# Block-sparse attention and a gated MLP on one core: two key loads change queues, pair 0's keys come in two parts, and the written order is a new one

## The chip, the cores and the metric

The kernel runs on one core of one Trainium2 chip. The metric is device microseconds of one execution, from the first instruction to the last store's arrival. Of the kernel before, three timed runs are given, with a median of 262.63 us (262.12 to 263.25). A core has a matrix engine (TensorE, PE in the profile), VectorE (DVE), ScalarE (ACT), GpSimd (POOL) and SyncE (SP). Each works through its own list of instructions in order. DMA transfers are issued from SP, ACT or POOL; an issue takes time on the list of the engine that issues it.

## The reference: what is computed

```python
# attention: batch 4, 8 heads, 768 positions, head width 64, blocks of 32
scores = scale * q @ k.T                       # per batch and head
mask = neighbours(+-1 block) | first/last block row or column | 3 sampled key blocks per query block
scores = where(mask, scores, -1e9)
attn = exp(scores - max); attn /= attn.sum(-1) + 1e-9
a = attn @ v
# MLP on the 3072 tokens, width 512, hidden width 2048
x = a.transpose(0, 2, 1, 3).reshape(3072, 512)
h = x @ w_in
out = (h / (1 + exp(-beta * h))) @ w_out       # float32
```

The mask is the same for every batch and head; it depends on `sampled_blocks`, a list of 24 x 3 integers that is read from memory.

## The kernel before, in words

**Tiling.** Two heads make a pair; there are 16 pairs (4 batches x 4). A pair's queries come in two tiles, one of 256 and one of 512, and a pair with one of its query tiles is called a unit: units 0 to 3 are the first 256 queries of pairs 0 to 3, units 4 to 7 their other 512, and so on to unit 31. Keys come in six chunks of 128. A unit has score steps (`sc` in `tile_steps`): a step is a double PSUM bank with 1024 columns. In units 0 to 3 a step covers two key chunks, so such a unit has three steps. ScalarE takes the exponential of each step (`ex`, tile `et`). VectorE multiplies the result with the 0/1 mask (`mk`). TensorE forms the weighted values (`av`), VectorE normalises (`norm`), and the result is turned into `x`.

**Masks in the first units.** In units 0 to 3 the mask isn't multiplied in. There TensorE adds -30000 to masked scores before the score product, with a one-hot matrix (`onehot`) against `shut_qk`. So those scores need `onehot`, `shut_qk`, and the turned keys `kX` and queries `qX`.

**Loads and turns.** A load (`add_load`) brings fp32 keys, queries or values into a staging tile (`st`, or `es`, which lies in the later `g` tiles). A cast makes fp16 of them (VectorE or GpSimd). For the first four pairs TensorE turns chunks of 128 by 128, and VectorE or ScalarE copies the turned chunks out of PSUM. Later pairs are turned by a DMA. `IN_PARTS` cuts the keys of pairs 0 and 1 into parts. `SPLIT_Q` cuts the queries of these pairs: first the 256 that units 0 and 1 need, then the rest (`add_rest`). One load, the one that `BESIDE` names, is issued by ScalarE; the others are issued by SP.

**The mask's own chain.** `emit_first` issues the load of the sampled list on ScalarE's queue and makes `identity`, the index tables and `onehot`. In `add_mask`, three VectorE instructions (`mb`) make the block mask from the list, a matmul (`mt`) spreads it, a copy (`mtc`) makes `mask_q`, and `neg` makes `shut_qk`. Three matmuls (`km`) and three copies (`kmc`) make the full mask `mask01`, which units from 4 on use. VectorE's list begins with `mb`.

**The MLP.** For each group of 256 or 512 tokens there are 16 hidden products (`hp`). ScalarE takes a tanh (`th`), VectorE multiplies (`gm`, tile `g`), and output products (`pr`) follow in a scheme with seven half-size products, whose sums on VectorE are `sg`; weight differences for them (`tw`, tile `w_mix`) are made once. `w_in` and `w_out` are loaded by GpSimd after the load that `GATE` names has landed.

**What sets the order.** `STEPS` is the order, written out by hand or by a search: `35S4` is node 35 on SP with buffer 4; the letters P, A, D, G, S stand for TensorE, ScalarE, VectorE, GpSimd and SP, and a number after a colon names a second TensorE node that shares the array with this one, each in one half of its rows (`in_halves`). Nodes are numbered in the order in which `add` makes them. The order fixes each engine's list; waits come from what a node reads and writes. Durations given to `add` and the times given as `at=` served the search and aren't in the program.

In the order before, SP's list starts: first queries of pair 1 (128 KB), keys of pair 1 chunks 0-1 (128 KB), all queries of pair 2 (384 KB), rest of pair 0's queries (256 KB), keys of pair 0 chunks 0-1 and 2-3 (128 KB each), first queries of pair 0 (128 KB), keys of pair 0 chunks 4-5 (128 KB), keys of pairs 2 and 3, queries of pair 3, `beta`, values. ScalarE's queue has the sampled list, then keys of pair 1 chunks 2-5 (256 KB). TensorE's list starts: `mt`, `km` for two groups, turns of pair 1's keys 2-5, keys 0-1 and queries, the third `km`, three score steps of unit 1, turns for pair 0 and of pair 2's queries, score steps of unit 0. ScalarE's starts: `onehot`, `mask_q`, `shut_qk`, two `kmc`, a copy of pair 1's keys, the third `kmc`, two exponentials of unit 1, a copy of pair 0's keys, the third exponential of unit 1, three of unit 0. Its first exponential takes the second score step that TensorE makes.

In the profile all instructions that are issued through the recording wrapper stand at one line, L200; they are told apart by their tiles. L362, L510, L392, L378 and L366 to L394 are in `add_load` and `emit_first`.

Of the kernel before, what the change touches and what calls it, by code (L numbers as in the profile page):

```python
# [43 lines left out]
0D 1P0 3A 4P7 8P6 2A 5A 9A 35S4 31S0 32D0 36D1 39S 40D 41P5 49S1 65S4 13S1 33P6 37P1 34A2 42D 6P5  # L44
7A 38D 21S 17S3 25S 96P3 94P1 95Ae 50D1 66G6 14G2 92P0 22D 18G3 26G 45S0 55S2 23P4 15P2 16D1 24D
59S3 10S 43S5 97A0 27P3 19P5 20D 29S4 28A 46G5 53S6 93A1 51P2 80P2 84P3 67P0 47P3 81A3 56G5 73G
82P2 74G 48D0 52D 60D1 68D 57P1 58D3 85A2 44G0 83A5 108P1 109Ac 106P3 107A6 104P2 61P1 62D 30D2
105A4 98P1 99P 116P3 87P0:86 100D0 101D0 117A8 63S7 75G 76G 69S8 54D1 118P1 188P2 189A9 86P 88D4
89D3 120P3 70G6 77G 78G 110P0 111P 112D2 11P4 12D 113D4 64D3 121A1 90P6 197P2 119Aa 194P0 79G
122P1 123P 91D0 124D4 198A3 195Ab 125D3 71P7 72D 191P2 192Ae 114P2 203P0 212P3 213A0 200P2 115D  # L50
190D 196D 201A1 204Aa 215P1 102P7 103D 126P6 127D 214D 193D 199D 149P5 128P4 216Ac 150A2 129A5
137P0 205D 202D 138A0 131P1 140P2 134P3 146P7 143P6 130D1 151D 217D 227P2 141A3 135A1 147A4 144A6
148D 145D 136D 132A5 228A2 218P3 219A4 161P3 167P4 158P5 162A1 168A4 159A2 139D 133D 229D 142D
220D 163D 155P2 224P3 156A3 225Ad 206P0:207 169D 160D 221P2 157D 222A8 226D 207P 244P1 245Ab 208Da
223D 209D4 164P6 173P7 170P4 165A3 246D 152P5 250P0 166D 171A1 174A4 230P1:231 153A0 251A7 175D
247P3 248A6 231P 154D 236S2 239S5 240D0 172D 288P0 232D1 259P2 260A1 256P3 237G3 238S1 233D1 257Ae
242S6 241S 268S7 176P23:182 276P2 277A2 252D 182P 183P:177 279P2 289Ac 285P3 280A5 177P 178P:184
286A3 258D 261D 253P2 271S3 249D 278D 291P0 356D 254Aa 357D 360D 281D 290D 255D 274S8 300S0 282P3
184P 179P 210P4 185P 283A0 292A4 287D 284D 293D 262P0:263 269G1 358D 361D 359D 211A1 180A1 186A0
# [63 lines left out]
1289D 1181S 1180S 1294A0 1296D 1299P 1301P 1302A1 1300D 1297D 1298D 1303P 1304D 1305P 1306D 1313S  # L123
1312S 1307A 1311D 1308P 1309A 1314S
"""
N_PEMASK = 4
ROWS6 = False
N_XPE = 8
SHUT = 30000.0
# [104 lines left out]
def kernel(  # L234
# [11 lines left out]
    nc = tc.nc  # L246
# [111 lines left out]
    def emit_first():  # L358
# [4 lines left out]
        for load in beside:  # L363
            load()
# [721 lines left out]
```

## Time and profile before

| what | value |
|---|---|
| median of three runs | 262.63 us (262.12 to 263.25) |
| the profiled execution's own time | 262.88 us |
| its span, first to last instruction | 261.1 us |
| TensorE busy | 249.6 us, 3767 matmuls |
| VectorE busy | 226.2 us, 445 instructions |
| ScalarE busy | 213.7 us, 288 instructions |
| GpSimd busy | 34.8 us, 50 instructions |
| moved by DMA | 36.81 MB, 141 GB/s over the span |

The profile shows one execution. Times in a timeline are microseconds from the start of the span; one line can stand for several instructions of one kind, with the first start and the time from there to the last end. Text in square brackets is idle time before the instruction and what ended it. Busy time of TensorE is modelled, so a busy TensorE isn't a TensorE at its peak.

### The profile page before, as it was taken

To read this page: it belongs to the slowest core of one execution; us is meant where nothing else is said; L and a number is where in the kernel's file an instruction comes from. 1 tells how busy PE (TensorE), PEld (TensorE's weight loads), DVE (VectorE), ACT (ScalarE), POOL (GpSimd) and SP (SyncE) were. 2 spreads that over 40 slices of the span, in tenths; PEclk is the share of its full clock that TensorE was granted. 3 is DMA by queue.
4 is the path that set the end of the run, shared out by engine and by line. 5 is a ranking of instruction groups with operands and counts; after the bars stand their busy time and mean duration, and the time that the engine had idled before them with its cause. 6 is when DMAs were issued, how large, how long until landed. Compare 5 with 4: busy or idle time off the path is not lost.

```text
span 261.1 us, 8802 instructions
## 1 busy us (share of the span) xinstructions
PE 249.6 (96%) x3767; PEld 171.8 (66%) x3767; DVE 226.2 (87%) x445; ACT 213.7 (82%) x288; POOL 34.8 (13%) x50
## 2 busy tenths in 40 slices
PE   5998799999989999999999999999999999999995
PEld 1675575564467976468876457856757986568894
DVE  4366998988999999989999999999999888589683
ACT  5699999999999997899898989975899874675241
POOL 3346001045220005210300200001100000000000
PEclk9999999999999999999999999999999999999999
DMA  6999994969756599931933999460050314100042
GB/s 202 340 342 175 207 198 85 280 167 262 178 194 189 175 121 246 172 133 35 261 83 73 251 147 253 57 137 0 3 183 4 22 23 173 22 3 0 3 160 81
DMA packets 50154, 36.81 MB, mean 141 GB/s; under 512 B 29748, under 2 KB 46660, under 8 KB 50116
## 3 DMA queue, kind: packets, MB, share of 16 engines
q1 hardware_dynamic: 46128, 31.80, 48.8%
q0 software_dynamic: 3680, 4.19, 9.8%
q8 instruction: 29, 0.48, 0.8%
q10 hardware_dynamic: 308, 0.26, 0.3%
q14 instruction: 9, 0.07, 0.1%
HBM read 27.27 MB, written 6.29 MB: 129 GB/s over the span
## 4 chain that ended last, share of the span: by engine, by line
PE 83%; DVE 11%; DMA 1%; ACT 1%; issue 1%; POOL 1%; SPq 0%; DVEq 0%; ACTq 0%
PE sc L200 83%; DVE et L200 5%; DVE g L200 3%; DMA st<-in_k_dram 1%; DVE xst L200 1%; ACT et L200 1%; DVE s L200 1%; DVE recip L200 0%; POOL s L200 0%; POOL va L200 0%; DVE kX L200 0%; ACT t_sb L200 0%; DVE va L200 0%; DVE x L200 0%; SPq L510 0%
## 5 line engine op out<-in xcount | busy, mean ns | idle before, releaser
L200 ACT ACTIVATE et<-sc 128x1024 f16<-128x1024 f32 x144 | 139.8, 1035 | 10.0 <-PE sc L200 8.5
L200 PE MATMUL sc<-x,w_in_sb 128*128 128x512 f16 (+2 forms) x504 | 92.1, 352 | 1.1 <-ACT et L200 0.5
L200 DVE TENSOR_TENSOR et<-et,mask 128x960 f16<-128x960 f16 x132 | 83.2, 670 | 1.4 <-ACT et L200 1.2
L200 ACT ACTIVATE t_sb<-sc,beta_c_sb 128x512 f16<-128x512 f32 (+1 forms) x112 | 65.1, 641 | 21.4 <-PE sc L200 19.4
L200 DVE SCALAR_TENSOR_TENSOR g<-t_sb,sc 128x512 f16<-128x512 f16 (+1 forms) x112 | 63.5, 606 | 7.8 <-ACT t_sb L200 7.3
L200 PEld LDWEIGHTS <-w_in_sb 128*128 128x128 f16 (+1 forms) x504 | 42.9, 97 | 37.5 <-issue 4.7
L200 PEld LDWEIGHTS <-g 64*128 64x128 f16 (+1 forms) x700 | 49.1, 96 | 15.2 <-issue 3.3
L200 PE MATMUL sc<-w_out_sb,g 64*128 64x256 f16 (+3 forms) x568 | 55.6, 281 | 0.5 <-DVE xst L200 0.3
L200 PE MATMUL sc<-qX,kX 64*128 64x256 f16 (+1 forms) x384 | 50.6, 328 | 1.4 <-DVE g L200 0.8
L200 PEld LDWEIGHTS <-et 64*128 64x128 f16 (+1 forms) x1776 | 41.7, 95 | 8.6 <-issue 1.4
L200 PE MATMUL sc<-va,et 64*128 64x65 f16 (+1 forms) x1776 | 44.3, 191 | 0.8 <-DVE xst L200 0.3
L200 PEld LDWEIGHTS <-kX 64*128 64x128 f16 x384 | 19.7, 95 | 12.5 <-issue 7.5
L200 POOL CAST s<-st 128x768 f16<-128x768 f32 (+2 forms) x17 | 15.1, 905 | 87.4 <-PE sc L200 34.5
L200 PEld LDWEIGHTS <-s 64*128 64x128 f16 (+1 forms) x320 | 22.0, 97 | 6.0 <-issue 1.7
L200 PE MATMUL sc<-w_mix,s 64*128 64x256 f16 (+1 forms) x272 | 23.6, 270 | 0.0
L200 DVE TENSOR_TENSOR xst<-sc,recip 128x256 f16<-128x256 f32 (+1 forms) x32 | 17.8, 557 | 0.9
L200 POOL CAST va<-st 128x768 f16<-128x768 f32 x10 | 9.6, 968 | 59.0 <-DVE g L200 32.0
L200 ACT COPY osb<-sc 128x512 f32<-128x512 f32 (+3 forms) x19 | 10.0, 539 | 8.5 <-PE sc L200 7.5
L200 PE MATMUL sc<-w_mix,g 64*128 64x256 f16 (+3 forms) x128 | 15.6, 264 | 0.0
L200 DVE TENSOR_TENSOR osb<-osb,sc 128x512 f32<-128x512 f32 (+2 forms) x19 | 11.7, 618 | 2.6 <-PE sc L200 1.5
L200 DVE RECIPROCAL recip<-sc 128x4 f32<-128x4 f32 (+1 forms) x32 | 6.2, 193 | 8.0 <-PE sc L200 7.7
L200 DVE CAST s<-st 128x768 f16<-128x768 f32 (+2 forms) x15 | 7.7, 522 | 2.0 <-DMA st<-in_k_dram 2.0
(60 smaller groups left out, 94.8 us busy)
## 6 DMA issues: line engine op xcount, KB each, us to landing
out_dram<-osb SPq DMA_DIRECT2D x23, 256.0 KB, 2.4
st<-in_k_dram SPq DMA_DIRECT2D x12, 384.0 KB, 4.9
st<-in_q_dram SPq DMA_DIRECT2D x12, 384.0 KB, 5.1
st<-in_v_dram SPq DMA_DIRECT2D x12, 384.0 KB, 4.5
g<-in_v_dram SPq DMA_DIRECT2D x4, 384.0 KB, 6.9
w_in_sb<-in_moe_w_in_dram POOLq DMA_DIRECT2D x2, 512.0 KB, 7.1
w_in_sb<-in_moe_w_in_dram POOLq DMA_DIRECT2D x1, 1024.0 KB, 10.7
w_out_sb<-in_moe_w_out_dram POOLq DMA_DIRECT2D x2, 512.0 KB, 12.9
```

The lines of the kernel that those rows point to most:

```text
L200: r = f(*a, **kw)
```

## The change

The loads of the first key chunks (0-1) of pairs 1 and 0 are issued by ScalarE, in this sequence: keys of pair 1, the sampled list, keys of pair 0. The load of pair 1's chunks 2-5, which ScalarE issued, goes to SP. Pair 0's keys come in two parts (chunks 0-1 and 2-5) and not in three, so one load, one cast, one turn and one copy fewer are there, and the node numbers above that point go down by four. The copy that makes `onehot` moves from ScalarE to GpSimd, ahead of the small `ident32` cast. The rest of the queries of pairs 0 and 1 goes into the staging tile of the first part, and no longer into one of its own. `shut_qk` is made 384 columns wide (it was 128) and lies in the `s` tile, which nothing uses before the MLP; the first units still use its first 128 columns. `PE_MASKED` names the same units 0 to 3 with all their steps. The mask copies may no longer go to GpSimd (none did).

`STEPS` is a new order. SP now starts: keys of pair 1 chunks 2-5 (256 KB), first queries of pair 1 (128 KB), keys of pair 2 (384 KB), first queries of pair 0 (128 KB), keys of pair 0 chunks 2-5 (256 KB), queries of pair 3, queries of pair 2, keys of pair 3, rest of pair 0's queries, values, rest of pair 1's, `beta`. TensorE starts: `mt`, turns of pair 1's keys 0-1, keys 2-5 and queries, three `km`, score steps of unit 1 (the first of them on chunks 0-1), turns of pair 0's keys 2-5 (four chunks), keys 0-1 (two), queries (two), of pair 2's keys (six), score steps of unit 0. ScalarE starts: `mask_q`, `shut_qk`, copies of pair 1's keys 0-1 and 2-5, one `kmc`, two exponentials of unit 1, the copy of pair 0's keys 0-1, the third of unit 1, three of unit 0; its first exponential takes the first score step. VectorE starts: `mb`, casts of pair 1's keys 0-1, keys 2-5 and queries, the copy of the queries, the cast of pair 2's keys, one `kmc`, the cast of pair 0's keys 2-5, another `kmc`. GpSimd casts pair 0's queries and first keys.

Further on, TensorE's list keeps nearly the order that it had: the pairs of nodes that run in half arrays are the same and in the same sequence, but for the weighted values of unit 0, which no longer share the array (41 pairs, 42 before). VectorE has 19 casts (22 before), GpSimd 33 (31 before). The casts of the keys for units 6 and 8 are now on VectorE (`265D3`, `417D3`), and one of the weight differences, `355D`, stands a few places later; several casts of units 13 to 23 have left VectorE. At the very end the narrow last product (`1306P5`, node 1310 before) stands after the wide one.

```diff
-0D 1P0 3A 4P7 8P6 2A 5A 9A 35S4 31S0 32D0 36D1 39S 40D 41P5 49S1 65S4 13S1 33P6 37P1 34A2 42D 6P5
-7A 38D 21S 17S3 25S 96P3 94P1 95Ae 50D1 66G6 14G2 92P0 22D 18G3 26G 45S0 55S2 23P4 15P2 16D1 24D
+27S0 35S 0D 1P0 28D0 29P7 36D 37P2 31S4 13S1 41S0 3A 2A 32D5 33P4 30A2 34D 17S3 21S 55S3 45S1 18G4
+14G1 4P0 6P1 8P3 38A 51S2 7A 88P3 90P2 89A0 42D2 5D 91A8 22D 9D 46G3 69G 70G 92P0 23P2 15P3 19P4
...
+181P 176A0 264S2 267S6 270S4 408P3 393P2 258P0:259 182A1 280D 354D 357D 265D3 358D 291P1:290 259P
...
+312D 316P2 317A2 313P0 424P3 337P13:319 271G2 395D 407D 417D3 314A4 425A2 318D 430P2 319P 431A3
...
+1304P 1308S 1306P5 1305A 1307D 1310S
...
-N_PEMASK = 4
+PE_MASKED = {0: 6, 1: 6, 2: 6, 3: 6}
-BESIDE = ("k", 1, 2)
-COPY384 = {"ACT": 395, "DVE": 465, "POOL": 480}
-EARLY = ("k2", "q2", "k3", "q3", "v0", "v1", "v2", "v3", "r1")
+BESIDE = (("k", 1, 0), ("k", 0, 0))
+COPY384 = {"ACT": 395, "DVE": 465}
+EARLY = ("k2", "q2", "k3", "q3", "v0", "v1", "v2", "v3")
-IN_PARTS = {0: (0, 2, 4, 6), 1: (0, 2, 6)}
+IN_PARTS = {0: (0, 2, 6), 1: (0, 2, 6)}
...
-    shut_qk = persist.tile([P, P], FP16, name="shut_qk")
+    shut_qk = T["s"][0].rearrange("p a f q -> p (a f q)")[:, 0:NG * P]
...
+        beside[0]()
         nc.scalar.dma_start(out=sb_i32, in_=sb_lo)
-        for load in beside:
-            load()
+        for i in range(1, len(BESIDE)):
+            beside[i]()
...
+        nc.gpsimd.tensor_copy(out=onehot, in_=onehot_n.rearrange("b p g -> b g p"))
         nc.gpsimd.tensor_copy(out=ident32, in_=identity[0:16, 0:16])
...
-        nc.scalar.copy(out=onehot, in_=onehot_n.rearrange("b p g -> b g p"))
...
-                act.activation(out=shut_qk, in_=at(tb)[:, 0:P], func=AF.Copy, bias=-SHUT,
+                act.activation(out=shut_qk, in_=at(tb)[:, 0:NG * P], func=AF.Copy, bias=-SHUT,
                                scale=SHUT)
...
-        st, s16 = at_work or (staging(f"{nm}{x}" if lo == 0 else f"r{x}"), Buf("s16"))
-        load = add_load(nm, x, st, lo, hi, gate, lo > 0 if at_work else None)
+        st, s16 = at_work or (staging(f"{nm}{x}"), Buf("s16"))
+        more = lo > 0 if at_work else None
+        if nm == "q":
+            st, more = rest_of.setdefault(x, st), lo > 0
+        load = add_load(nm, x, st, lo, hi, gate, more)
...
-                                rhs=shut_qk[r].unsqueeze(1).to_broadcast([D, CG, P]),
+                                rhs=shut_qk[r, q0 // CG:(q0 + n) // CG].rearrange(
+                                    "b (g p) -> b g p", p=P).unsqueeze(1).to_broadcast(
+                                        [D, CG, ng, P]),
...
-            steps, ets = tile_steps(x, q0, n, i * NPAIR + j < N_PEMASK)
+            steps, ets = tile_steps(x, q0, n, PE_MASKED.get(i * NPAIR + j, 0))
```

More of the change, by code (lines that the diff above doesn't have):

```diff
@@ L470 @@
     prep = {}
[L472 to L473 removed]
+    w_in_of, w_out_of, loads, rest_of, begun = {}, {}, {}, {}, {}
+    last_load, begin, early_casts, beside = [], [], [], {}
     def add_weights():
```

189 lines of the change are left out of this document (94 added, 95 removed).

## The prediction

> **What bounds the kernel now.** I read the page first, for the chain of work that ended last; then the busy time by stretches, because a share over the whole span mixes stages; then the timeline of the first 14 us, where the change lies; then the landing times of single loads.
>
> ```profile
> span 261.1 us, 8802 instructions
> PE 83%; DVE 11%; DMA 1%; ACT 1%; issue 1%; POOL 1%; SPq 0%; DVEq 0%; ACTq 0%
> ```
>
> ```profile
> 0.00:9.40 9.40, 6.48 (x34) 2.96 (x36) 4.72 (x21) 4.14 (x8) 3.60 (x16) 1.00 0.80 236
> 9.40:40.00 30.60, 27.30 (x489) 20.16 (x483) 22.13 (x57) 30.28 (x43) 8.29 (x12) 1.00 1.14 245
> 40.00:100.00 60.00, 58.65 (x1053) 36.98 (x1047) 56.67 (x103) 57.59 (x71) 11.90 (x13) 1.00 0.77 180
> 120.00:258.00 138.00, 137.78 (x1986) 99.94 (x1983) 123.71 (x233) 104.41 (x144) 6.07 (x6) 1.00 0.39 90
> ```
>
> Columns of the stretches: length, then busy time of PE, PEld, DVE, ACT, POOL, clock, DMA share, GB/s. The chain is TensorE's for 83% of the span and VectorE's for 11%. TensorE idles 2.9 us before 9.4, 3.3 us from there to 40, and 1.35 us from 40 to 100. From 9.4 to 40 the full engine is ScalarE (30.28 of 30.60): it takes exponentials one after another. After 120 TensorE is full (137.78 of 138). So what ScalarE gains at its first exponentials moves the train to 40 us, and the rest follows if nothing in between takes it back. TensorE's work stays the same: the same matmuls, masked units and turned chunks.
>
> ```profile
> 0.74 0.66 ACTq L362 DMA_DIRECT2D sb_i<-in_sampled_blocks_dram  x1
> 1.26 0.45 SPq L510 DMA_DIRECT2D st<-in_k_dram  x1
> 1.42 0.41 ACTq L510 DMA_DIRECT2D st<-in_k_dram  x1
> 1.75 1.06 POOL L378 COPY g<-identity 64x384 f16<-64x384 f16 x2
> 1.86 1.28 ACT L392 ACT_TABLE_LOAD   x1 [1.86 <-issue]
> 2.25 0.16 DVE L200 CAST sb_f<-sb_i 24x3 f32<-24x3 int32 x1 [0.21 <-DMA sb_i<-in_sampled_blocks_dram]
> 3.16 0.51 ACT L392 COPY onehot<-g 128x384 f16<-128x384 f16 x1
> 3.32 0.50 PE L200 MATMUL sc<-g,mask 24*128 24x384 f16 x1 [0.24 <-DVE mask L200]
> 3.85 0.47 ACT L200 CAST mask_q<-sc 24x384 f16<-24x384 f32 x1 [0.18 <-PE sc L200]
> 4.22 0.26 ACT L200 ACTIVATE shut_qk<-sc 128x128 f16<-128x128 f32 x1
> 4.37 0.79 PE L200 MATMUL sc<-mask_q,onehot 24*128 24x384 f16 x2 [0.56 <-ACT mask_q L200]
> 5.12 0.83 DVE L200 CAST s<-st 128x256 f16<-128x256 f32 x3 [1.86 <-DMA st<-in_k_dram]
> 6.86 0.37 ACT L200 COPY kX<-sc 128x256 f16<-128x256 f16 x1 [1.12 <-PE sc L200]
> 7.28 0.55 DVE L200 CAST s<-g 128x768 f16<-128x768 f32 x1
> 7.53 0.40 PE L200 MATMUL sc<-shut_qk,onehot 64*128 64x256 f16 x2
> 7.99 0.72 DVE L200 CAST s<-st 128x256 f16<-128x256 f32 x1 [0.16 <-DMA st<-in_k_dram]
> 8.36 0.42 PE L200 MATMUL sc<-shut_qk,onehot 64*128 64x256 f16 x2
> 9.46 1.94 ACT L200 ACTIVATE et<-sc 128x1024 f16<-128x1024 f32 x2 [1.34 <-PE sc L200]
> 10.21 0.92 PE L200 MATMUL sc<-identity,s 128*128 128x128 f16 x8
> 11.67 2.86 ACT L200 ACTIVATE et<-sc 128x1024 f16<-128x1024 f32 x3
> 12.01 0.27 PE L200 MATMUL sc<-shut_qk,onehot 64*128 64x256 f16 x2
> 12.76 0.73 PE L200 MATMUL sc<-identity,s 128*128 128x128 f16 x10
> ```
>
> The gate of the start is the landing of pair 1's first keys: VectorE waits 1.86 us for it, until 5.12. Casts, turns and copies of 512 KB of pair 1 follow, and the first score step begins at 7.53. The second begins at 8.36, so a step takes 0.83; the first exponential, at 9.46, takes that second step: 1.10 after its begin. The fourth exponential, unit 0's first, stands at 11.67 + 0.97 = 12.64.
>
> ```profile
> st<-in_q_dram SPq DMA_DIRECT2D x1, 128.0 KB, 2.3
> st<-in_k_dram SPq DMA_DIRECT2D x1, 128.0 KB, 3.8
> st<-in_k_dram ACTq DMA_DIRECT2D x1, 256.0 KB, 3.9
> g<-in_q_dram SPq DMA_DIRECT2D x1, 384.0 KB, 4.6
> ```
>
> These are the first three loads of SP's queue (issued at 0.74, 1.26 and 1.76) and the key load of ScalarE's, with microseconds from issue to landing: 3.04, 5.06, 6.36 and 5.32.
>
> **The change part by part.**
>
> *Three issues on ScalarE.* 0.46 more than before (an issue of 128 KB on SP took 0.45), so the table load ends near 3.6 and not 3.14. ScalarE's next work comes at 5.1 (below): costs nothing; uncovered it would be 0.46.
>
> *The one-hot copy.* ScalarE loses 0.51, which nobody waited for. GpSimd does half of the partitions in 0.53 (1.06 for two), so it ends at 3.3 to 3.9, if the other read pattern doubles it. The first reader is a `km` at 5.85. Nothing.
>
> *The sampled list.* It is issued at 1.2 in place of 0.74. VectorE began on it 1.51 after the issue. Below that is 2.7; above, behind 128 KB on the same queue, 1.2 + 3.8 = 5.0. I take 3.5, nearer to the list's own row, since its packets are few. The three `mb` instructions take 1.0 (from 2.25 to just before the matmul at 3.32), and behind them on VectorE's list wait all the casts: 4.5. The spreading matmul adds 0.55, `mask_q` 0.47 from 5.1, and `shut_qk`, now as wide as `mask_q`, 0.47 in place of 0.26: 6.0. The copy of the first keys is then done at 6.4.
>
> *Pair 1's loads.* The last one needed is now the queries, second on SP behind 256 KB. Before, 256 KB of SP's queue had landed at 5.06 and 640 KB at 6.36; 384 KB lie between, at 5.5, less up to 0.5 because two queues start at 0.74. I take 5.3; the ends are 1.26 + 2.3 = 3.6 and 1.26 + 4.6 = 5.9. The keys' casts are done by then (4.5 plus two thirds of 0.83). The cast of the queries ends at 5.6, their two turns (0.115 each, by 0.92 for eight) at 5.85, and three `km` 0.3 apart (0.79 for two against 0.50 for the one matmul of that width at 3.32) put the first score step at 6.8. The copies (6.3 for the queries, 6.4 for the keys, at 0.37) are earlier. First exponential: 6.8 + 1.1 = 7.9, which is 1.56 earlier than 9.46. The order gives 0.83 of that, as ScalarE takes the first step instead of the second.
>
> *Pair 0.* Now its stage is next to be late. Ahead of and with its keys 2-5, SP's queue holds 256 + 128 + 384 + 128 + 256 = 1152 KB, as it held before with its chunks 2-3 (128 + 128 + 384 + 256 + 128 + 128), and ScalarE's queue 256 KB both times: landing near 8.0, as the wait before the cast at 7.99 shows. The wider cast takes 0.42 to 0.72, to 8.7. TensorE is with unit 1 until 6.8 + 3 x 0.83 = 9.3. Then it turns 14 chunks at 0.115, among them six of pair 2's keys, and starts unit 0 at 10.9: its exponential can start at 12.0. ScalarE waits for the copy of pair 0's first keys (10.2 to 10.6), and ends unit 1's third at 11.6; so it waits again. Fourth exponential: 12.0 against 12.64. Of 1.56 us, 0.65 are left. One load, cast, turn and copy fewer for pair 0 change nothing else.
>
> *Shared staging for the rest of the queries.* Their loads now stand ninth and sixteenth on SP; units 4 and 5 want them, of whose order nothing comes before the exponentials above. Nothing; the cover is ScalarE's train.
>
> *The order further on.* The half arrays lost by unit 0's weighted values lie where ScalarE is the limit: nothing. The doubtful place is where the chain runs through VectorE without a break:
>
> ```profile
> 62.92 1.29 DVE g L200 x2
> ...
> 71.27 0.60 DVE s L200
> ...
> 74.84 0.84 POOL va L200
> ```
>
> Into it come the cast for unit 8 (0.55 to 0.56) and a weight difference (0.60, by the sum at 71.27): +1.16 at most. Out of it can go the value cast on GpSimd, 0.84, which now stands earlier in its list. I take the middle, nothing. Four casts that leave VectorE beyond 105 us lie beside a full TensorE: nothing. At the end the narrow product is last, and a VectorE addition of 64 columns follows it where ScalarE's 192-column copy stood:
>
> ```profile
> 257.95 0.32 ACT L200 COPY osb<-sc 128x192 f32<-128x192 f32 x1 [0.91 <-PE sc L200]
> ```
>
> That is between the copy's 0.32 won and as much lost; taken as nothing.
>
> *Sum:* -0.65 against the profiled execution's 262.88 (span 261.1), so 262.2. The median of the runs is 0.25 below that execution: 261.9 to 262.0. I give 261.9.
>
> [...]
>
> **The rivals.**
>
> *The clock rises earlier (faster).* Two score matmuls take 0.42 until the 9s and 0.27 at 12.01; turns go from 0.115 to 0.073 (0.73 for ten). TensorE would now work almost without a break from about 4.6, where it had idled until the casts of 5.12 were in. If the rate doubles by 8.5, unit 1's third step takes 0.45, the 14 turns 1.0, unit 0 starts at 10.0, and ScalarE, not waiting, has its fourth exponential at 11.15: 1.5 earlier, 261.1. Against it: TensorE was busy for 6.48 of the first 9.4 us before, too, and the rate rose only between 10.21 and 12.01.
> [...]
>
> *Pair 0's keys are late (no change).* Each 0.1 that the keys land after 8.7 is lost; at 9.35 the gain is gone: 262.6. For it: they are one transfer now, so all four chunks wait for the last. Against: the byte count above.
>
> *VectorE takes the gain back (slower).* Casts of the keys for units 6 and 8 stand on its list now, and whatever it waits for there, its products and masks wait too. GpSimd, which made them, could wait for a load at no cost:
>
> ```profile
> 58.90 2.18 POOL L200 CAST s<-st 128x768 f16<-128x768 f32 x2 [2.42 <-DMA st<-in_q_dram]
> ```
>
> With 1.16 of added work and half such a wait, 1.2, the sum is -0.65 + 2.36: 264.3. It decides as soon as work and wait on the chain exceed 0.65. Against it: the masks of unit 8 now stand first in that stretch, so TensorE's next weighted values hang less on its end.
>
> **How the numbers follow.** Forecast 0.45, earlier clock 0.20, late keys 0.13, VectorE 0.22. A measurement of this kernel tells about 0.5%, 1.3 us, from no change: below 261.3 is faster, above 263.9 slower. The forecast's own range is 261.2 to 262.6. Faster: 0.8 of the clock case and 0.3 of the forecast, 0.30. Slower: 0.8 of the VectorE case and a little of the others, 0.20. Within: 0.50. The range runs from 260.6 (the clock case with the queries landing 0.5 earlier, well above their lower end of 3.6) to 264.4, a little past the VectorE case.
>
> **What the changed profile would show.** Right: VectorE's first mask instruction between 2.7 and 4, the first score step near 6.8, the first exponential near 7.9, a short wait of ScalarE before unit 0, the fourth exponential near 12.0, ScalarE full to 40, and a chain that is TensorE's from 120 on. Wrong: the list or the queries landing after 6; scores at 0.27 a pair already before 9; VectorE idle before a cast between 48 and 70 us; or new idle time of TensorE between 40 and 120, above the 1.35 us it has there up to 100 now.

## The result, and the profile after

The changed kernel takes 265.98 us in the median (265.81 to 266.18, four runs); the kernel before, on the same chip, takes 262.73 us (262.12 to 263.25, four runs). The ratio is 1.0125, with a 95% interval of 1.0101 to 1.0149: slower by 1.2%. The forecast was 261.9 us, and its range ended at 264.4. The profiled execution of the changed kernel took 266.12 us, with a span of 264.3; that is 3.24 us more than the 262.88 of the profiled execution before (spans: 3.2).

These are lines of the page of the changed kernel: busy time, a DMA queue (packets, MB, share), and the chain of work that ended last.

```profile
span 264.3 us, 8745 instructions
PE 251.2 (95%) x3743; PEld 172.3 (65%) x3743; DVE 228.2 (86%) x442; ACT 212.4 (80%) x286; POOL 36.5 (14%) x53
...
q8 instruction: 29, 0.48, 0.8%
...
PE 78%; DVE 14%; ACT 2%; issue 2%; DMA 1%; ACTq 0%; DVEq 0%
```

VectorE's part of the chain rose from 11% to 14%, and TensorE's fell from 83% to 78%, with 24 matmuls fewer (3743, 3767 before). The queue named "instruction" comes up again below: 29 packets with 0.48 MB, 16,384 bytes each by the packet records.

The timeline of the start of the changed kernel:

```profile
0.73 0.48 ACTq L510 DMA_DIRECT2D st<-in_k_dram  x1
1.24 0.73 ACTq L363 DMA_DIRECT2D sb_i<-in_sampled_blocks_dram  x1
2.43 1.28 ACT L200 ACT_TABLE_LOAD   x1 [2.43 <-issue]
2.86 0.50 POOL L384 COPY onehot<-g 128x384 f16<-128x384 f16 x1
4.63 0.16 DVE L200 CAST sb_f<-sb_i 24x3 f32<-24x3 int32 x1 [2.59 <-DMA sb_i<-in_sampled_blocks_dram]
5.35 0.81 DVE L200 CAST s<-st 128x256 f16<-128x256 f32 x3
6.01 0.47 ACT L200 CAST mask_q<-sc 24x384 f16<-24x384 f32 x1 [2.30 <-PE sc L200]
7.96 0.40 PE L200 MATMUL sc<-s,onehot 64*128 64x256 f16 x2
8.12 0.50 DVE L200 CAST s<-st 128x512 f16<-128x512 f32 x1
9.04 1.94 ACT L200 ACTIVATE et<-sc 128x1024 f16<-128x1024 f32 x2 [0.81 <-PE sc L200]
10.64 1.67 PE L200 MATMUL sc<-identity,s 128*128 128x128 f16 x14
13.32 2.86 ACT L200 ACTIVATE et<-sc 128x1024 f16<-128x1024 f32 x3 [0.53 <-PE sc L200]
```

The gate of the start is now the sampled list. VectorE waits 2.59 us for it, until 4.63, and its three casts of pair 1 stand behind it and then wait for nothing. The first exponential is at 9.04 (9.46 before), but the fourth is at 13.32, where the prediction had 12.0. Before, the fourth stands at 12.58 in the trace (the 12.64 of the prediction is a sum), so it is 0.74 late; by 25 us the exponentials are 0.68 behind those of before.

What TensorE waited for from 16 us to the end, in the waits of the changed kernel (total, times, longest):

```profile
PE sc L200 <- issue: 2.1, 3, 0.8
...
PE sc L200 <- DVE g L200: 0.7, 2, 0.5
```

The same query on the kernel before has this line:

```profile
PE sc L200 <- issue: 0.2, 1, 0.2
```

Now there are three pauses of 0.6 to 0.8 us that no engine, semaphore or load of the program ended, as far as the profile shows. One of them in the timeline of TensorE:

```profile
77.07 0.93 PE L200 MATMUL sc<-va,et 64*128 64x65 f16 x48 [0.23 <-DVE xst L200]
77.83 0.39 PE L200 MATMUL sc<-qX,kX 64*128 64x512 f16 x2
78.12 0.74 PE L200 MATMUL sc<-va,et 64*128 64x65 f16 x36
79.64 0.36 PE L200 MATMUL sc<-va,et 64*128 64x65 f16 x12 [0.78 <-issue]
```

TensorE stops in the middle of 48 equal matmuls, after 36 of them. The other two pauses are of 0.61 at 40.78 and 0.68 at 169.91. The three stand on the chain of waits too, as "issue".

So the 3.2 us of the two traces come from: the start, 0.68 (at 25 us); the pauses, 0.61 + 0.78 + 0.68 - 0.15 = 1.92; and the rest, 0.6, of which nothing can be seen in a wait.

### The profile page after: what moved, and what is told of

The parts are those of the page before. It is cut to its first block, busy times and chain, and to the rows that moved or that the text cites. A ratio compares the mean times of both kernels' runs of the same rounds, so it can differ in the third digit from the quotient of the medians.

```text
span 264.3 us, 8745 instructions
## 1 busy us (share of the span) xinstructions
PE 251.2 (95%) x3743; PEld 172.3 (65%) x3743; DVE 228.2 (86%) x442; ACT 212.4 (80%) x286; POOL 36.5 (14%) x53
## 4 chain that ended last, share of the span: by engine, by line
PE 78%; DVE 14%; ACT 2%; issue 2%; DMA 1%; ACTq 0%; DVEq 0%
PE sc L200 78%; DVE et L200 5%; DVE g L200 4%; DVE xst L200 2%; ACT et L200 1%; DMA sb_i<-in_sampled_blocks_dram 1%; ACT t_sb L200 1%; DVE w_out_sb L200 1%; DVE recip L200 1%; DVE s L200 1%; DVE osb L200 0%; DVE va L200 0%; DVE kX L200 0%; ACTq L510 0%; DVE x L200 0%
## 5 line engine op out<-in xcount | busy, mean ns | idle before, releaser
L200 DVE TENSOR_TENSOR et<-et,mask 128x960 f16<-128x960 f16 x132 | 84.1, 674 | 0.7 <-ACT et L200 0.6
L200 PEld LDWEIGHTS <-et 64*128 64x128 f16 (+1 forms) x1752 | 41.6, 95 | 11.8 <-issue 4.3
L200 POOL CAST s<-st 128x768 f16<-128x768 f32 (+1 forms) x19 | 17.0, 903 | 96.3 <-PE sc L200 51.7
L200 DVE TENSOR_TENSOR osb<-osb,sc 128x512 f32<-128x512 f32 (+2 forms) x19 | 11.6, 615 | 4.1 <-ACT osb L200 1.9
L200 POOL CAST va<-st 128x768 f16<-128x768 f32 x10 | 8.7, 884 | 46.7 <-PE sc L200 23.9
L200 DVE TENSOR_TENSOR g<-g,s 128x1024 f16<-128x1024 f16 (+1 forms) x12 | 8.1, 691 | 0.0
## 6 DMA issues: line engine op xcount, KB each, us to landing
w_in_sb<-in_moe_w_in_dram POOLq DMA_DIRECT2D x1, 1024.0 KB, 11.8
```

The costliest lines, as they stand in the source:

```text
L200: r = f(*a, **kw)
```

## The experiments

All times are medians; the kernel before was run beside each group, with 262.79, 262.52, 262.48 and 262.63 us. The groups ran on different chips, and every trace is of one execution. "Place" is an instruction's place in TensorE's own list, counted from the list's first over all its records: matmuls, weight loads, and the 18 to 22 semaphore and drain instructions among them. Records that start within a few ns of each other can change places by one.

### What the pauses have in common

Counted in this way, the pauses of the changed kernel stand at places 962, 2241 and 5057, and the one of the kernel before (0.15 at 39.36 us) at 962 too. Divided by 256 each leaves 193 or 194. TensorE's list has about 7500 instructions, and 29 packets on the queue "instruction" make some 259 of them for each. That gave the theory of the first experiments: TensorE's instructions arrive in blocks of 256, by DMA, and a block is late where TensorE runs through the one ahead of it too fast. The stretches where it stops are dense: 48 matmuls with 64 rows and their 48 weight loads pass in 0.93 us.

What the traces show of such blocks is 16,384 bytes in each of the 29 packets and pauses whose places differ by multiples of 256. That one packet brings one block is the author's estimate, from the 259 instructions for each packet. In what follows a block is 256 places of TensorE's list, and its first place is 193 or 194 above a multiple of 256.

Unit 0's weighted values gave up their half arrays, which takes 48 instructions out of the list near its begin. So everything behind them stands at another place against the blocks' ends than before.

### The list first on its queue

```diff
-        beside[0]()
         nc.scalar.dma_start(out=sb_i32, in_=sb_lo)
+        beside[0]()
```

> The changed kernel, with the sampled list issued first on ScalarE's queue and pair 1's first keys second. Theory (late list): VectorE's mask work starts near 2.3 instead of 4.63, the first score step near 6.8 instead of 7.96, unit 0's first exponential near 12.0 instead of 13.32, and the time falls by about 1.3 us to 264.7. Rival (pair 0's stage or something further on sets the end, and the list only looked like the gate): the list moves, the exponential of unit 0 stays within 0.3 of 13.3, and the time stays at 266. The three pauses of TensorE without a releaser (0.61 at 40.8, 0.78 at 79.6, 0.68 at 169.9) stay in both, since the instruction list of TensorE is the same.

264.99 us (264.34 to 265.39), ratio to before 1.0095 (1.0066 to 1.0124), and 0.99 below the changed kernel. Lines of the timeline of this kernel:

```profile
2.25 0.16 DVE L200 CAST sb_f<-sb_i 24x3 f32<-24x3 int32 x1 [0.21 <-DMA sb_i<-in_sampled_blocks_dram]
4.50 0.83 DVE L200 CAST s<-st 128x256 f16<-128x256 f32 x3 [1.24 <-DMA st<-in_k_dram]
...
7.01 0.40 PE L200 MATMUL sc<-s,onehot 64*128 64x256 f16 x2
...
8.08 1.94 ACT L200 ACTIVATE et<-sc 128x1024 f16<-128x1024 f32 x2 [0.81 <-PE sc L200]
9.68 1.42 PE L200 MATMUL sc<-identity,s 128*128 128x128 f16 x14
...
12.16 1.94 ACT L200 ACTIVATE et<-sc 128x1024 f16<-128x1024 f32 x2 [0.32 <-PE sc L200]
```

The list is there at 2.25, as before, and the start runs nearly as the prediction had it: first score step 7.01 (6.8 predicted), first exponential 8.08 (7.9), fourth 12.16 (12.0). The three pauses stay, with 0.59, 0.49 and 0.65. The late list is one of the causes, worth 1.0 in the medians, where 1.3 was expected.

### Forty-eight idle instructions more in the changed kernel

```diff
         emit_zeros(4, 7, 512)
+        for _ in range(24):
+            pe.matmul(T["sc"][3][0:32, 1, 0:1], lhsT=warm[:, 0:32], rhs=warm[:, 0:1], start=True, stop=True)
```

> The changed kernel with 24 one-column matmuls added behind the four zero matmuls, while TensorE waits for the list: 48 instructions more on TensorE's list, no other change. Theory (instruction blocks): TensorE's pauses lie at places 962, 2241 and 5057 of its list, all 193 or 194 above a multiple of 256; shifted by 48, the places fall on wider work, the pauses go, and the time falls by about 2.0 us to 264.0. Rival (the order's own waits or DMA load make the pauses): they stay at the same matmuls at 40.8, 79.6 and 169.9, and the time stays at 266, or grows by the filler.

264.14 us (263.69 to 264.88), ratio to before 1.0066 (1.0044 to 1.0089): 1.84 us faster than the changed kernel, by instructions that do nothing. The fourth exponential is at 13.32, as without them. The pauses at 40.8 and 169.9 us are gone; one of 0.89 is left at 78.39, at place 2241 of the new list. The idle time put down to "issue" fell by 1.18 only (2.07 to 0.89). A pause costs more than the idle time that is recorded for it: across the 0.78 at 79.64 the changed kernel's exponentials fell back by 1.08 (1.16 to 2.24 behind those of before, from 69 to 85 us of the kernel before), where the same order without pauses lost nothing. In four traces a pause near 78 us of 0.49 to 0.89 went with 0.63 to 1.08.

### Sixty idle instructions more in the kernel before

```diff
         emit_zeros(4, 7, 512)
+        for _ in range(30):
+            pe.matmul(T["sc"][3][0:32, 1, 0:1], lhsT=warm[:, 0:32], rhs=warm[:, 0:1], start=True, stop=True)
```

> The kernel before with 30 one-column matmuls behind its zero matmuls: 60 instructions more. Theory (instruction blocks): block ends now fall at place 1669 of the old list, at 54 us, 256 instructions after a place that lies only 2.2 us earlier, and at 2181 (76 us) and 6021 (197.7 us) with 3.7 to 3.8 us: new pauses of TensorE there, 1 to 3 us in all, and 263.8 to 265.5. Rival: the filler costs nothing or its own time at the start (under 0.5), no pauses, 262.7 to 263.2.

264.29 us (263.48 to 265.25), ratio 1.0066 (1.0041 to 1.0091): the kernel before gets slower by 1.5 us, though its start was 0.3 earlier. Pauses of 0.86 and 0.34 came up at places 1730 and 2242, two of the three that were named:

```profile
54.82 0.33 PE L200 MATMUL sc<-va,et 64*128 64x65 f16 x10 [0.86 <-issue]
```

The third, near 197 us, did not come. There the packet had begun 2.4 us before TensorE entered the block ahead, at a DMA share of 0.40 over that block, against 0.42 for the block ahead of the second. So a block's end and a dense stretch are not enough.

### Both repairs in the changed kernel

The edits of the first two experiments together.

> Both edits to the changed kernel: list first and 24 one-column matmuls. Theories together: -1.3 and -2.0, 262.6 to 262.9, level with the kernel before. If either is wrong, what is missing tells which: 264.0 without the list's part, 264.7 without the blocks' part. The filler may now stand in the way of the mask matmul, since the list lands earlier: up to 1 us back.

263.65 us (263.14 to 265.15), ratio 1.0045 (1.0023 to 1.0067). That is 2.33 below the changed kernel, but it missed the expected value by 0.75 to 1.05: the pause at place 2241 stays, with 0.89, and the kernel is 0.86 above the one before although its start is earlier. So something else costs time, too. (The trace is of the slowest of its eight executions, 265.15 us.)

### Half arrays for unit 0 again

```diff
-10S 82P2 83P
+10S 82P2:83 83P
```

> The changed kernel with one thing put back: unit 0's weighted values run in half arrays again, so that TensorE's list has the 48 instructions (24 weight loads, 24 matmuls) more that the kernel before had, from there on. Nothing is added that does no work. Theory (TensorE's instructions come in blocks of 256, and the pauses stand where a dense stretch meets a block's end): the same picture as with the 24 idle one-column matmuls, 264.1 us (263.5 to 264.7): pauses near 40.8 and 169.9 gone, one of 0.6 to 0.9 near 78.4 at place 2241 of the list; the fourth exponential still near 13.3. Rival (the idle matmuls helped in another way, by keeping TensorE awake at the start, and the half arrays are free as the prediction had it): 266.0, with the three pauses of 0.6 to 0.8 where they were.

264.19 us (263.93 to 264.47), ratio 1.0072 (1.0055 to 1.0090). That is the time with the 24 idle matmuls, and again one pause alone, 0.58 at 77.70, place 2241. This undoes a part of the change itself and adds nothing idle. With the idle matmuls, which move the list and nothing else, it says that most of the 1.8 us is the price of where the list stands against the blocks. What the half arrays save by themselves is the subject of a later experiment.

### Fewer bytes in the changed kernel

```diff
+            whole = hi - lo < NC or x < 4 or id(at(st)) not in filled
+            some = slice(0, P if whole else 16)
+            if hi - lo == NC:
+                filled.add(id(at(st)))
-            (nc.scalar if other else nc.sync).dma_start(out=at(st)[:, :, lo * D:hi * D], in_=rows[:, :, lo * D:hi * D])
+            (nc.scalar if other else nc.sync).dma_start(out=at(st)[some, :, lo * D:hi * D], in_=rows[some, :, lo * D:hi * D])
```

> The changed kernel, order and list of TensorE untouched, but the loads of pairs 8 to 15, and of the values of pairs 5 to 7, bring 16 of the 128 partitions only, 48 KB instead of 384 (the rest of a tile keeps older data, so these pairs' part of the output is not computed from their own inputs). Theory (a block of instructions is itself fetched by DMA, and is late only where the DMA engines are full): the pauses near 79.6 and 169.9 shrink under 0.2 us, the one near 40.8, before any cut load, stays at 0.5 to 0.7; 264.7 us (264.2 to 265.2). Rival (the place in the list alone makes the pause): all three stay at 0.5 to 0.8 and the time between 265.6 and 266.2.

264.55 us (264.50 to 264.77), ratio 1.0088 (1.0071 to 1.0104). Two pauses are gone, and the one at 40.55 is as large as ever (0.77). Stretches that hold the last block before each of the three places, first of the changed kernel, then of this one (length, busy TensorE, clock, DMA share, GB/s):

```profile
75.20:79.70 4.50, 2.97 (x139) 1.00 1.04 271
164.70:170.00 5.30, 4.62 (x137) 1.00 1.02 296
36.00:40.80 4.80, 4.19 (x112) 1.00 1.27 185
```

```profile
74.70:78.40 3.70, 2.94 (x144) 1.00 0.29 64
164.00:168.40 4.40, 4.40 (x134) 1.00 0.36 35
36.00:40.60 4.60, 3.83 (x108) 1.00 1.26 191
```

The same list of TensorE, the same places. Where the DMA share fell from about 1.0 to 0.3, the pause went; where it stayed at 1.26, the pause stayed. In the DMA records of the changed kernel the packet for the block that starts at place 2241 begins 1.73 us after TensorE entered the block ahead, and 2.79 before the first instruction of the new one; here it begins after 0.87, and the new block is entered 2.69 later, without a pause. The time from packet to use is nearly the same; what the cut loads made earlier is the packet's begin. (Which packet belongs to which block is counted off in order; the trace doesn't name it.)

### The new start, the old order behind it

After the first 140 steps of the changed order stands the order of the kernel before, with two slots of `et` renamed; the list is issued first, and unit 0 has its half arrays.

> The changed start with the sampled list issued first on ScalarE's queue, the changed order for its first 140 steps, and from there the order of the kernel before; unit 0's weighted values in half arrays, so TensorE's list stands against the block ends as it did before. Theory (the start is worth what the prediction's sum said once the list is early, and what the changed kernel loses later belongs to its order and its block ends): fourth exponential at 12.1 to 12.2, pauses of 0.2 together as before, 262.3 us (261.8 to 262.8), 0.5 below the kernel before. Rival (the start's lead is given back in any body, since TensorE is full from 120 us on and other loads land elsewhere): 262.8 to 263.3, no better than before.

262.36 us (261.48 to 262.67, twelve runs) against 262.52: ratio 0.9992 (0.9976 to 1.0008). No pause at all. The profiled execution has a span of 260.5, 0.6 below that of before, and the lead of its exponentials over before is 0.44 at 40 us and 0.64 from 100 us to the end; in the medians only 0.16 of it is seen, which the interval doesn't tell from nothing. The fourth exponential came at 12.46, not at 12.1 to 12.2: the 14 turns took 1.68 us here and 1.42 in the kernel with the list first, and two score matmuls behind them took 0.39 to 0.44 until 12.4 us here and 0.28 to 0.29 from 11.03 us on there.

### Pair 2's turns behind unit 0

```diff
-43P5 16A1 93A4 24D 20D 80P3 81Ae 56D6 44D0 52D0 61S 39S5 40G2 25S4 76P1 78P0 47P4 57P5 77A1 53P6
+16A1 93A4 24D 20D 80P3 81Ae 56D6 52D0 61S 39S5 40G2 25S4 76P1 78P0 43P5 44D0 47P4 57P6 77A1 53P7
```

> The same as the kernel with the changed start and the old order behind it, but the turns of pair 2's keys, six chunks that stand ahead of unit 0's score steps on TensorE, move behind them. Theory (the fourth exponential waits for TensorE's 14 turns): with eight turns of 0.115 to 0.12 it comes 0.4 to 0.6 earlier, at 11.6 to 11.8, and 0.3 to 0.5 of it reach the end: 261.9 us (261.4 to 262.4). Rival (unit 2, which needs those turns, waits in its place): the exponentials of unit 0 come earlier, but those of unit 2 no earlier or later than in the other kernel, and the time is the same as there or up to 0.4 more.

263.03 us (262.59 to 264.01, twelve runs), ratio 1.0026 (1.0014 to 1.0038): 0.67 above the kernel with the turns ahead, the rival, and more than the 0.4 that it allowed. ScalarE's exponentials, first with the turns ahead (the kernel of the experiment above), then with the turns behind:

```profile
12.46 6.67 ACT L198 ACTIVATE et<-sc 128x1024 f16<-128x1024 f32 x7 [0.64 <-PE sc L198]
...
19.57 1.02 ACT L198 ACTIVATE et<-sc 128x1024 f16<-128x1024 f32 x1 [0.44 <-PE sc L198]
```

```profile
11.48 0.28 PE L198 MATMUL sc<-qX,kX 64*128 64x256 f16 x2 [0.79 <-DVE qX L198]
...
12.03 3.96 ACT L198 ACTIVATE et<-sc 128x1024 f16<-128x1024 f32 x4 [0.32 <-PE sc L198]
...
15.68 0.29 PE L198 MATMUL sc<-s,onehot 64*128 64x256 f16 x2 [0.76 <-DVE qX L198]
...
16.33 3.10 ACT L198 ACTIVATE et<-sc 128x1024 f16<-128x1024 f32 x3 [0.35 <-PE sc L198]
...
19.87 1.02 ACT L198 ACTIVATE et<-sc 128x1024 f16<-128x1024 f32 x1 [0.44 <-PE sc L198]
```

The fourth exponential is at 12.03, not at 11.6 to 11.8: with the turns out of the way TensorE waits 0.79 for VectorE's copy of pair 0's queries. 0.43 is won there, some of it by faster matmuls: two score matmuls took 0.28 or 0.29 from 10.41 us on in this trace, and 0.39 to 0.44 until 12.4 us in the other. Then unit 2's score steps wait for copies on VectorE, ScalarE waits 0.35 once more, and at the eighth exponential the kernel is 0.24 behind, from the tenth on 0.30. What was taken from one wait went to the next.

### One part alone: the kernel before without unit 0's half arrays

```diff
-87P0:86 100D0 101D0 117A8 63S7 75G 76G 69S8 54D1 118P1 188P2 189A9 86P
+86P0 100D0 101D0 117A8 63S7 75G 76G 69S8 54D1 118P1 188P2 189A9 87P
```

> The kernel before with one part of the change alone: unit 0's weighted values no longer run in half arrays, so TensorE's list is 48 instructions shorter from about 18 us on, and every later instruction stands 48 places further ahead of its block's end. Theory (pauses at the ends of blocks of 256 instructions where the stretch is dense and the DMA engines full): pauses at places 2289 (near 77 us, where 256 instructions take 3.64 us) of 0.4 to 0.9, at 5105 (near 167 us, 4.35) of 0.1 to 0.6 and at 1009 (near 39.6 us, 4.52) of 0.1 to 0.5; 263.4 to 264.2 us, most likely 263.7. Rival (the half arrays of unit 0 are worth nothing either way, as the prediction had it): 262.6, no pause above 0.2.

264.00 us (263.68 to 264.43), ratio 1.0060 (1.0041 to 1.0079). The time is as expected, and not quite for the reason given. The pause that was named at 39.6 us came (0.29, at 40.62), those near 77 and 167 us did not; instead one of 0.61 stands at 54.74, at place 1474, again a block's end. Pauses add 0.29 + 0.61 - 0.15 = 0.75. And 0.75 were lost before the first of them, by 25 us (0.08 of it already at the first exponential), in the stage where ScalarE takes one exponential after another: from the first of 12 matmuls over the whole array to the next score matmul 0.49 us pass, where 24 halves let 0.42 pass, this happens twice, and ScalarE waits. Lines of the kernel before, then of this one:

```profile
15.60 11.56 ACT L200 ACTIVATE et<-sc 128x1024 f16<-128x1024 f32 x12 [0.15 <-PE sc L200]
...
18.13 0.54 PE L200 MATMUL sc<-va,et 64*128 64x65 f16 x24
18.55 0.29 PE L200 MATMUL sc<-shut_qk,onehot 64*128 64x256 f16 x2
```

```profile
18.36 0.55 PE L200 MATMUL sc<-va,et 128*128 128x65 f16 x12
18.85 0.28 PE L200 MATMUL sc<-shut_qk,onehot 64*128 64x256 f16 x2
...
19.72 4.89 ACT L200 ACTIVATE et<-sc 128x1024 f16<-128x1024 f32 x5 [0.20 <-PE sc L200]
...
24.90 3.01 ACT L200 ACTIVATE et<-sc 128x1024 f16<-128x1024 f32 x3 [0.29 <-PE sc L200]
```

Without half arrays the train of twelve exponentials breaks twice (0.20 and 0.29). In the changed kernel this direct price is small: at 25 us it stands at +0.68 against before, and with the half arrays at +0.25; of the 0.43 between them, 0.33 is already there at the fourth exponential (13.32 and 12.99), ahead of the half arrays. There the rate of the matmuls differs: the 14 turns took 1.67 us in the trace of the changed kernel and 1.21 in the one with the half arrays.

### The late list in the kernel before

```diff
-        nc.scalar.dma_start(out=sb_i32, in_=sb_lo)
         for load in beside:
             load()
+        nc.scalar.dma_start(out=sb_i32, in_=sb_lo)
```

> The kernel before with one thing changed: on ScalarE's queue the sampled list is issued behind the 256 KB of pair 1's keys instead of ahead of them. Theory (a small transfer on a queue lands only with the large one ahead of it, and VectorE's casts stand behind the mask it starts): the list lands at 4.8 to 5.8 instead of 2.25, the first score step moves from 7.53 to 8.3 to 9.0, the fourth exponential from 12.64 to 13.3 to 13.9; 263.4 us (263.1 to 263.9). Rival (the start has slack, since pair 1's keys land at 5.1 in any case and pair 0's at 8.0): 262.6, the fourth exponential within 0.2 of 12.64.

264.10 us (264.04 to 264.69), ratio 1.0068 (1.0048 to 1.0089). Lines of its timeline:

```profile
4.66 0.15 DVE L200 CAST sb_f<-sb_i 24x3 f32<-24x3 int32 x1 [2.62 <-DMA sb_i<-in_sampled_blocks_dram]
...
8.92 0.40 PE L200 MATMUL sc<-shut_qk,onehot 64*128 64x256 f16 x2
...
10.85 1.94 ACT L200 ACTIVATE et<-sc 128x1024 f16<-128x1024 f32 x2 [1.34 <-PE sc L200]
...
12.96 2.86 ACT L200 ACTIVATE et<-sc 128x1024 f16<-128x1024 f32 x3
```

One swapped line in the old kernel makes the first score step 1.39 later and the fourth exponential 1.3 (13.9 by the sum at 12.96). The end moved by 1.6, more than expected, since the pause at place 962 grew from 0.15 to 0.49. The list came at 4.66 behind 256 KB (4.8 to 5.8 expected), and at 4.63 in the changed kernel behind 128 KB: between these two its delay doesn't grow with the bytes ahead of it on the queue. In both it is also issued 0.5 later than before (1.24 against 0.74), and packets of SP's loads run from 1.84 on; no run separates the later issue from the place on the queue.

### What the order behind the start costs

The changed order whole, with list first, half arrays and cut loads; and the new start with the old order and the same cut loads.

> The changed kernel's whole order with the sampled list first, unit 0's weighted values in half arrays, and the loads of pairs 8 to 15 and the values of pairs 5 to 7 cut to 16 partitions of 128 (these pairs' part of the output is then not computed from their own inputs): the start as the prediction had it, and nothing left that makes a block of instructions late. Theory (the order behind the start costs something of its own, beside the pauses): no pause above 0.2, 262.9 us (262.5 to 263.2), 0.4 to 0.7 above the same kernel with the old order behind the start. Rival (start and pauses are all there is): within 0.2 of that kernel, 262.1 to 262.5.

> The changed start with the list first and the old order behind it, with the same loads cut to 16 partitions (the same part of the output left out). It had no pause before the cut, so both theories expect 262.3 us (262.0 to 262.6): fewer bytes alone are worth nothing. If it comes below 261.9, the loads cost something else than late instructions, and the step of the other cut kernels has to be read again.

263.12 us (262.88 to 263.41) and 262.20 us (261.41 to 262.99), twelve runs each; ratios to before 1.0012 (0.9996 to 1.0029) and 0.9986 (0.9966 to 1.0006). Neither has a pause. The second shows that fewer bytes alone gain no more than 0.16. So the changed order behind the start costs 0.9 by itself, more than the 0.4 to 0.7 expected. The table compares the starts of the same exponentials and tanhs, kernel against the kernel before (medians of eight in a row from that time on, worked out from the traces, in us):

| at (before) | changed | list first | half arrays again | new start, old order | new order, nothing late |
|---|---|---|---|---|---|
| 25 | +0.68 | -0.55 | +0.25 | -0.11 | -0.19 |
| 39 | +1.04 | -0.20 | -0.11 | -0.44 | -0.53 |
| 63 | +1.07 | -0.18 | -0.15 | -0.44 | -0.56 |
| 69 | +1.16 | -0.08 | -0.06 | -0.44 | -0.47 |
| 85 | +2.24 | +0.55 | +0.68 | -0.44 | -0.49 |
| 90 | +2.49 | +0.79 | +0.92 | -0.44 | -0.25 |
| 105 | +2.15 | +0.43 | +0.83 | -0.64 | -0.23 |
| 157 | +2.19 | +0.46 | +0.92 | -0.64 | +0.09 |
| 206 | +3.69 | +1.94 | +1.57 | -0.63 | +0.74 |
| 235 | +1.43 | -0.31 | -0.69 | -0.63 | -1.52 |
| 240 | +3.18 | +1.42 | +1.05 | -0.63 | +0.23 |

In the last column the order falls back by 0.2 from 85 to 90, by 0.3 between 105 and 157 and by 0.65 between 181 and 206. Single rows can't be taken for losses, though: the same column reads -1.52 at 235 and +0.23 at 240, and the three other kernels with the new order make the same jump. What is left at the end is +0.23 against -0.63 with the old order: 0.86, which agrees with the 0.9 of the medians. From 120 to 200 TensorE is busy for 79.8 of 80 us in that kernel and 79.9 with the old order and cut loads, so no wait of TensorE shows the loss there. Over the whole traced executions it is busy for 251.3 us in that kernel and for 250.6 with the new start and the old order, with 3767 matmuls each. So most of the 0.9 seems to lie in TensorE's own work, in how its instructions follow each other; which of them, and where, isn't settled.

No version beat the kernel before by more than its measurement can tell: the two fastest, 0.9992 and 0.9986, have intervals that hold 1.

## Why the prediction was wrong, step by step

**The sampled list, "I take 3.5": the first step that failed.** Its bounds, 2.7 and 5.0, held the 4.63; the value taken between them was 1.13 too early. The choice "nearer to the list's own row, since its packets are few" was the mistake: a list of 0.6 KB behind one other load on the queue came 3.4 us after its issue, against 1.5 when first on it. The three mask instructions took 0.8 (1.0 predicted), `shut_qk` ended at 6.87 (6.0), the first score step came at 7.96 (6.8), the first exponential at 9.04 (7.9), the fourth at 13.32 (12.0).

Behind the list the chain of terms was nearly right: with the list early it gave 7.01 and 8.08, and a fourth exponential at 12.16, at 12.43 to 12.46 in three traces where the 14 turns took 1.68 us (1.42 in the first), and at 12.77 in a fifth. In all five VectorE's list stands still for pair 2's keys, whose cast is ahead of pair 0's: 1.0 to 1.1 us, and 1.84 in the fifth. The prediction had no such wait. Some of the agreement is luck. The loads of pair 1 had landed by 4.5 where 5.3 was taken, and the turns ended at 6.01 where 5.85 was taken; in the trace with 12.16, the turns for pair 0 took 1.42 in place of 1.61, and TensorE then waited 0.31 for VectorE's copy of the queries, a wait that the prediction didn't have. Against the 12.58 of before, the start with the list early was worth between -0.2 and 0.4 at the fourth exponential, not 0.65.

**"The half arrays lost by unit 0's weighted values lie where ScalarE is the limit: nothing": the second, and the larger.** The working looked at the time of these matmuls and not at their count. Their loss moves 7000 instructions by 48 places against the blocks, and the pauses cost at least 1.92 in the profiled execution; putting the half arrays back takes 1.79 off the median, and 48 idle instructions, which move the list alone, take 1.84 off. In the kernel before the same edit also made ScalarE wait, so even the cover that was named doesn't hold everywhere.

**"The order further on: nothing": the third.** With start and pauses taken out, 0.9 remain. They don't lie at the place that was doubted (0.1 from 63 to 69 us); where they do lie stays open.

**Pair 0's stage.** Right in the changed kernel. The keys of chunks 2-5 were there when VectorE came to them at 8.12, the turns took 1.67 for 14 (1.61 by 0.115), and ScalarE's fourth exponential followed the shifted first one: 13.32, where 12.0 + 1.16 is 13.16. That both came as worked out rests on 0.119 us a turn through all 14, near the 0.115 that the prediction took; in the trace with 12.16 it was 0.101 (1.42 for 14).

**What was costed at nothing at the start.** Right: the table load ended at 3.71 (3.6) and ScalarE's next work came at 6.01; GpSimd's copy took 0.50 and ended at 3.36, without the doubling. At the end VectorE's narrow addition closes 2.9 us before the span's end, where ScalarE's copy stood at 2.8: nothing, as taken.

**VectorE takes the gain back.** Hardly. Through 63 to 69 us, where the casts and the weight difference moved, the changed kernel lost 0.1, and the same order without pauses 0.1; TensorE's waits for VectorE's `g` fell to 0.7. The time lies on this rival's side without its mechanism.

**The clock rises earlier.** No: in the changed kernel's trace it rose later. Two score matmuls took 0.42 until 10.3 us and 0.28 or 0.29 only from 13.1, where before they took 0.42 until 9.9 and 0.27 or 0.28 from 11.8; the clock records begin, at the full clock, at 13.05 us (10.77 before). The moment differs between executions: with the same instructions up to there, the 14 turns took 1.67 us in the changed kernel, 1.61 in the one with fewer bytes and 1.21 in the one with the half arrays, and the fourth exponential came at 13.32, 13.08 and 12.99. What sets the moment, unbroken work of TensorE as this rival took it or something else, no run shows. So a difference of 0.2 or 0.3 us at the fourth exponential of two traces can come from this alone.

**Pair 0's keys are late.** No; see above.

**Pair 1's loads.** The last of them landed at 4.8, 0.5 before the 5.32 of before, and not at the 5.3 that the sum took. The time didn't follow, since the list was the gate by then. The list's own delay came with the second place on its queue and an issue 0.5 us later: 1.39 us at the first score step in the kernel before (8.92 against 7.53).

**The signs named.** Of the four that would show the prediction wrong, the last came: TensorE idles 3.11 us from 40 to 100 (60 less 56.89), above the 1.35 of before, and 1.39 of it are two pauses. That it would be a wait for nothing in the program wasn't thought of.

## What to carry to other kernels

Give the load that gates a chain the first place on its queue, above all when it is small: here nothing ahead of it was "hidden" (behind one other load the list came 3.4 us after its issue, first on the queue 1.5). When an edit adds or removes instructions of a dense engine, count them: before a stretch is called slower, look whether a wait is put down to "issue" and whether it stands at a fixed place modulo 256 in that engine's list (193 or 194 in all 16 pauses here); then compare orders only with the alignment made equal. And when the time moves the wrong way, put the new start before the old order: it splits a rewritten order into its parts in one run.

## What the runs showed of the hardware that was not expected

**Pauses at fixed places of TensorE's list.** Over all fourteen kernels, the two given ones and the experiments, 16 pauses of 0.15 us or more were put down to "issue" after the start, and all stand at places that leave 193 or 194 when divided by 256:

| kernel | pauses: us at (place) |
|---|---|
| before | 0.15 at 39.4 (962) |
| changed | 0.61 at 40.8 (962), 0.78 at 79.6 (2241), 0.68 at 169.9 (5057) |
| list first | 0.59 at 39.5 (962), 0.49 at 78.0 (2241), 0.65 at 168.2 (5057) |
| 48 idle instructions | 0.89 at 78.4 (2241) |
| before with 60 idle instructions | 0.86 at 54.8 (1730), 0.34 at 77.1 (2242) |
| both repairs | 0.89 at 77.6 (2241) |
| half arrays again | 0.58 at 77.7 (2241) |
| fewer bytes | 0.77 at 40.6 (962) |
| before without half arrays | 0.29 at 40.6 (962), 0.61 at 54.7 (1474) |
| before with the late list | 0.49 at 41.0 (962) |
| the other four | none |

Worked out from the records of these traces: in all 16 cases the packet with the next block began 0.6 to 3.2 us after TensorE entered the block ahead, and the first instruction of the next block came 2.2 to 2.95 us after that begin. TensorE ran through the block ahead in 2.4 to 4.9 us. The pause is what the first two make more than the third: 1.73 + 2.79 - 3.74 = 0.78 at place 2241 of the changed kernel. In twelve of the 16 the DMA share over the block ahead was 0.99 to 1.27, and the packet began 1.6 to 3.1 us after the entry. Near 77 us, with shares of 0.06 to 0.51, it began after 0.6 to 1.4 us in eight kernels, and blocks of 3.7 to 4.1 us passed there without a pause. The share isn't a rule, though: the other four pauses, in the kernel before with 60 idle instructions and in the one without half arrays, came at shares of 0.42 to 0.77, one of them with a packet as late as 3.2 us, and the new start with the old order ran through place 962 without a pause at a share of 1.12.

What makes a packet begin stays open. That TensorE's entry into the block ahead starts it doesn't come out of the records: over all 392 blocks that follow another, the packet began between 3.3 us before and 4.0 us after TensorE entered the block ahead, and before it in 97. (The records show when TensorE works on an instruction, not when it is read.)

**A small load behind others.** The list took 1.5 us from issue to use when first on its queue, and 3.4 behind 128 KB as well as behind 256 KB. The packet records show one likeness: the load ahead is 256 packets in both cases, of 512 and of 1024 bytes, and 161 and 142 of them had begun before the list's first. Whether the number of packets is what counts, or the later issue, stays open.
